# Folding a small block weight into a projection on Trainium2: row groups of 32 rows in place of 64

## The chip, the cores and the metric

The kernel runs on one core of a Trainium2 chip. The metric is the device time of one execution in microseconds (us): the median of the runs before the change is 219.45 us, over 3 runs from 219.3 to 219.51 us. One more execution was taken with the hardware profiler; every start, duration and wait below is from that one.

A core has five engines that matter here, each with a queue of its own that it works off in order: PE (TensorE, matrix products; its weight loads are listed apart as PEld), ACT (ScalarE), DVE (VectorE), POOL (GpSimd) and SP, which issues nearly all DMAs. Matrix products land in PSUM, which has eight banks of 512 float32 values per partition; ACT and DVE move results from there to SBUF.

## The reference, cut to what matters

```python
xn = _layernorm(x)                                   # 2048 tokens x 512
q, k, v = xn @ wqkv, split in 32 heads of 16
pq = einsum("bhsd,hdf->bhsf", q, w_phi)              # a 16x16 matrix for each head
pk = einsum("bhsd,hdf->bhsf", k, w_phi)
phi = concat([softmax(p), softmax(-p)])              # for q and for k
kv, z = sum over tokens of phi_k (x) v, and of phi_k
o = (phi_q @ kv) / (phi_q . z + 1e-6)
out = x + o @ wo + ((xn @ w_gate) * (xn @ w_up)) @ w_down
```

Since pq = (xn @ Wq) @ w_phi for each head, the kernel never forms q or k. It folds w_phi into the projection weights first: W' = Wq . blockdiag(w_phi) is 512x512, and pq = xn @ W'. The same is done for k. The change is in this fold.

## The kernel before, in words

Tokens are in 16 tiles of 128. The work is written as a list of steps (`_Sched.step` and `.dma`), each with its engine, its reads and writes, and a cost in nanoseconds. `_order` (L819) then plays a list schedule with these costs and with due times (`at`) for the DMAs, and fixes each engine's order: the engine takes the step that can start first, among equals the one of lowest `prio`, which is the order of writing unless given. A step marked urgent may be preferred if it is ready within 300 ns (50 ns on PE). `_emit_all` (L873) writes the queues and the semaphore waits. So a changed cost can move steps anywhere behind it.

The stages: layer norm of tiles 0 to 3 by hand (`emit_centred` L433, `emit_T` L494 with PE transposes, `emit_moments`, `emit_root` with POOL), v for these tiles (`k_pe` L574), then `make_wbd` (L408) and `wprime(1)` (L515), which folds for k. Then, tile by tile, pk = xn @ W' (`k_pk` L584), its exponentials (`emit_exp` L531), sums and norm (`k_norm` L589). The gated unit (`glu` L607: 56 units, each of two groups of four matmuls of 128x512, read out by ACT and DVE) has a low priority and fills PE wherever nothing else is ready. Late in the k stage `wprime(0)` folds for q; then come the q tiles (`q_pk` L667, `q_num` L689) with the output products (`final` L711) as filler.

The parts that the change touches:

- `make_wbd` (L408 to L414): four POOL operations, one for each block of 128 rows (eight heads), write wbd, 128 columns a block: two squares of 64x64, each with four heads' w_phi on its diagonal. Columns within a square are ordered with the head fastest (f, then head). The mask is bind8 (L395, L398), which is 1 where partition p belongs to head column p // 16.
- `wprime(w)` (L515 to L523): 32 matmuls. Each has 64 rows of the transposed weight wT as its stationary operand (64x128) and a 64x64 square of wbd as the moving one. The two halves h = 0, 1 of the partitions use the two row groups of the array and write to different PSUM banks, so four banks are filled. Its planned cost is set to 660 ns. Then four ACT copies of 512 columns each bring a bank into Wp, in runs of 64 columns.
- wT for k is loaded with a transposing DMA (L344, L379), w_phi by L376; wT for q is loaded at L781.
- The banks come from `next_a` (L489), a ring of banks 0 to 3 that `k_pe`, `k_pk` and `emit_kv` use too; `glu` has banks 4 to 7 in this time.
- `act_op` is L278 in the profile, matmuls L298, bind8's relatives on DVE are maskh (L403) and eps4 (L405).

Of the kernel before, what the change touches and what calls it, by code (L numbers as in the profile page):

```python
# [7 lines left out]
ACTF = mybir.ActivationFunctionType  # L8
ALU = mybir.AluOpType
AX = mybir.AxisListType  # L10
I32 = mybir.dt.int32

PE, ACT, DVE, POOL, SP = "PE", "ACT", "DVE", "POOL", "SP"
# [7 lines left out]
NQ = D // 128  # L21
# [160 lines left out]
def bass_parallel_sum__linear_kernel_hedgehog__glu_gated_bilinear__prompt_kernel(  # L182
    nc: bass.Bass,
    A_x: bass.AP,
    A_wqkv: bass.AP,
    A_w_phi: bass.AP,
    A_wo: bass.AP,
    B_x: bass.AP,
    B_w_gate: bass.AP,
    B_w_up: bass.AP,  # L190
    B_w_down: bass.AP,
    out: bass.AP,
):
    with ExitStack() as es:
        _build(nc, es, A_x, A_wqkv, A_w_phi, A_wo, B_w_gate, B_w_up, B_w_down, out)


def _build(nc, es, A_x, A_wqkv, A_w_phi, A_wo, B_w_gate, B_w_up, B_w_down, out):
# [4 lines left out]
    def alloc(name, nelem_bf16, at=None):  # L203
        if at is not None:
            layout[name] = at
            return at
        off = (cur[0] + 31) // 32 * 32
        layout[name] = off
        cur[0] = off + nelem_bf16
        return off  # L210
# [11 lines left out]
    alloc("wu", NQ * FF)  # L222
    alloc("wd", NF * 512)
    alloc("wphi", NQ * 16)
    alloc("wbd", NQ * 128)
    alloc("ident", 128)
    alloc("bind8", 8)
    alloc("maskh", 4)
    alloc("eps4", 2 * 4)
    o_vext = alloc("vext", NT * 8 * 66)  # L230
    o_ek = alloc("ek", NT * 1024)
# [27 lines left out]
    def sbv(name, lo, n):  # L259
        off = layout[name] + lo  # L260
        return arena[:, off:off + n]

    def sbf(name, lo_f32, n_f32):
        off = layout[name]
        return arena[:, off:off + 2 * (lo_f32 + n_f32)].bitcast(F32)[:, lo_f32:lo_f32 + n_f32]

    def bank(b, lo=0, n=512):
        return psum[:, b * 512 + lo: b * 512 + lo + n]

    sc = _Sched(nc)  # L270


    def act_op(out_ap, in_ap, func=ACTF.Copy, scale=1.0, bias=None, prio=None):
        def fn(e):
            kw = {}
            if bias is not None:
                kw["bias"] = bias
            return e.activation(out=out_ap, in_=in_ap, func=func, scale=scale, **kw)  # L278
        r = [in_ap]
        if isinstance(scale, bass.AP):  # L280
            r.append(scale)
        if isinstance(bias, bass.AP):
            r.append(bias)
        return sc.step(ACT, fn, reads=r, writes=[out_ap], cost=(50.0 if str(in_ap.tensor.name) == "ps" else 95.0) + 0.833 * in_ap.free_size(),
                       lat=180.0, prio=prio)

    def dve(fn, reads, writes, n, rate=1.0, fixed=65.0, prio=None):
        return sc.step(DVE, fn, reads=reads, writes=writes, cost=fixed + rate * n / 0.96, lat=150.0, prio=prio)

    def pool(fn, reads, writes, n, rate=1.8, fixed=130.0, prio=None):  # L290
        return sc.step(POOL, fn, reads=reads, writes=writes, cost=fixed + rate * n, lat=120.0, prio=prio)

    def mms(items, prio=None, cold=False):

        def fn(e):
            ins = None
            for o, l, r, a, z in items:
                ins = e.matmul(o, lhsT=l, rhs=r, start=a, stop=z)  # L298
            return ins
        reads = []  # L300
        writes = []
        c = 0.0
        for o, l, r, a, z in items:
            reads += [l, r]
            writes.append(o)
            c += max(25.0, o.free_size() / 2.4 + 2.3) * (1.92 if cold else 1.0)
        return sc.step(PE, fn, reads=reads, writes=writes, cost=c, lat=260.0, prio=prio)
# [4 lines left out]

    ident = sbv("ident", 0, 128)
    bind8 = sbv("bind8", 0, 8)
    maskh = sbv("maskh", 0, 4)
    eps4 = sbf("eps4", 0, 4)
    x_flat = A_x.flatten_outer_dims()
# [10 lines left out]
    wT_v = sbv("wT", 0, 2 * NQ * 512).rearrange("p (w j d) -> p w j d", w=2, j=NQ)  # L328
# [5 lines left out]
    wphi_v = sbv("wphi", 0, NQ * 16).rearrange("p (j f) -> p j f", j=NQ)  # L334
# [64 lines left out]
                                   pattern=[[16, 8]], channel_multiplier=-1), [bind8], [bind8], 30)  # L399
    vext_all = sbv("vext", 0, NT * 8 * 66).rearrange("p (t c j) -> p t c j", t=NT, c=8)  # L400
    pool(lambda e: e.memset(vext_all[:, :, :, 64:65], 1.0), [], [vext_all[:, :, :, 64:65]], 128)
    wbd_v = sbv("wbd", 0, NQ * 128).rearrange("p (j c) -> p j c", j=NQ)
    dve(lambda e: e.tensor_reduce(out=maskh, in_=ident.rearrange("p (f b) -> p b f", b=4), axis=AX.X, op=ALU.add),  # L403
        [ident], [maskh], 128)
    dve(lambda e: e.tensor_scalar(out=eps4, in0=maskh, scalar1=5e-7, scalar2=None, op0=ALU.mult),  # L405
        [maskh], [eps4], 4)

    def make_wbd():  # L408
        for jt in range(NQ):
            pool(lambda e, jt=jt: e.tensor_tensor(  # L410
                out=wbd_v[:, jt, :].rearrange("p (g f b) -> p g f b", g=2, b=4),
                in0=wphi_v[:, jt, None, :, None].to_broadcast([128, 2, 16, 4]),
                in1=bind8.rearrange("p (g b) -> p g b", g=2)[:, :, None, :].to_broadcast([128, 2, 16, 4]), op=ALU.mult),
                [bind8, wphi_v[:, jt, :]], [wbd_v[:, jt, :]], 128).deps.append(sc.by_eng[POOL][-2])  # L414


    stats_v = sbf("stats", 0, NT * 8).rearrange("p (t k) -> p t k", t=NT)
# [71 lines left out]
    def next_a():  # L489
        b = a_bank[0] % a_banks[0]  # L490
        a_bank[0] += 1
        return b
# [20 lines left out]
    Wp_v = sbv("Wp", 0, 2 * NQ * 512).rearrange("p (w q f) -> p w q f", w=2, q=NQ)  # L513

    def wprime(w):  # L515
        bs = [[next_a(), next_a()] for _ in range(2)]
        mms([(bank(bs[dt // 2][h], dt % 2 * 256 + jt * 64, 64), wT_v[64 * h:64 * h + 64, w, jt, dt * 128:(dt + 1) * 128],
              wbd_v[64 * h:64 * h + 64, jt, 64 * h:64 * h + 64], True, True)
             for dt in range(NQ) for jt in range(NQ) for h in range(2)]).cost = 660.0
        for d in range(2):  # L520
            for h in range(2):
                act_op(Wp_v[:, w, 2 * d:2 * d + 2, :].rearrange("p t (j c) -> p t j c", j=NQ)[:, :, :, 64 * h:64 * h + 64],
                       bank(bs[d][h]).rearrange("p (t j c) -> p t j c", t=2, j=NQ))  # L523


    sums_v = sbf("sums", 0, 3 * 64).rearrange("p (r k) -> p r k", r=3)
# [230 lines left out]
    for t in range(RAW):  # L757
# [8 lines left out]
        emit_root(t)  # L766
        k_pe(t)
    make_wbd()
    emit_squares()
    wprime(1)  # L770
    for b0 in range(0, NT, 4):
        if b0 < 12:
            ln(b0 + 4, 4)
        if b0 == 0:
            for load in [load_x(SP, 8, 8, 30000.0)] + load_gu(SP, 9, 5, 32000.0, 34000.0):
                load.deps.append(sc.by_eng[DVE][-1])
        if b0 == 4:
            load_later(lambda: load_w(SP, wd_v, B_w_down.rearrange("(f p) j -> p f j", p=128), 48000.0),
                       lambda: load_w(SP, wo_v, A_wo.rearrange("(q p) j -> p q j", p=128), 50000.0))
        if b0 == 8:  # L780
            load_wT(0, 0.0).deps.append(sc.by_eng[SP][-2])  # L781
            emit_kv(0)
            some_glu(99, 2)
        for t in range(b0, b0 + 4):
            k_pk(t)
            k_norm(t)
            if b0 < 8:
                some_glu(2, 1)
        if b0 < 12:
            for t in range(b0 + 4, b0 + 8):  # L790
                k_pe(t)
        if b0 == 8:
            some_glu(4, 3)
            wprime(0)
# [162 lines left out]
```

## Time and profile before

| What | Value |
|---|---|
| median of the runs | 219.45 us (219.3 to 219.51) |
| the profiled execution, its own time | 219.1 us |
| its span, first to last instruction | 217.9 us |
| PE busy | 213.2 us, 98% of the span, 1291 records |
| DVE busy | 187.1 us, 86% |
| ACT busy | 128.7 us, 59% |
| POOL busy | 10.8 us, 5% |
| granted TensorE clock | 1.00 |

The span is the time from the first instruction's start to the last one's end; the other 1.2 us of the execution's own time lie around it. Busy times are unions of the records of an engine. A matmul's record is longer than its share of the engine, since matmuls are pipelined: a 128x512 matmul has a record of 379 ns, while the next starts 216 ns after it. What counts on PE is therefore the time from start to start, called the pitch here. Some matmul records are missing from a trace, so a pitch of twice 216 ns is a lost record and not a pause.

"The chain of waits" is the page's fourth part: the work that ended last, followed back. "Groups by form" lists instructions of one line, engine and shape with their summed and mean time. "Windows" gives each engine's busy time in a stretch.

### The profile page before, as it was taken

The numbers are of one execution on the slowest core, as the hardware profiler recorded it, in microseconds if no ns is written. First come the engines' busy times: TensorE is split into PE (matmuls) and PEld (weight loads), VectorE is DVE, ScalarE is ACT, GpSimd is POOL, SyncE is SP. The second block draws the span as 40 slices with busy tenths as digits, with TensorE's granted clock in tenths as the row PEclk, the third lists the DMA queues.
The fourth block names the chain that finished last, engine by engine and source line by source line (L and its number), as shares of the span: only waits on it lengthen the run. The fifth ranks groups of instructions, "written<-read, shape, count | busy, mean of one in ns | idle before, by whom it ended". The sixth has DMA issues, their size and how long they took to land.

```text
span 217.9 us, 3623 instructions
## 1 busy us (share of the span) xinstructions
PE 213.2 (98%) x1291; PEld 104.4 (48%) x1314; DVE 187.1 (86%) x556; ACT 128.7 (59%) x223; POOL 10.8 (5%) x29
## 2 busy tenths in 40 slices
PE   7999999999999999999999999999999999999996
PEld 6444444444444554444446444444445444454544
DVE  3785999999999549999998799999999999995512
ACT  4668966548553399999884899795254531110000
POOL 2432000110000300000000000000000000000000
PEclk9999999999999999999999999999999999999999
DMA  5994690025900224000000005542681746447321
GB/s 167 321 280 106 164 317 5 0 48 130 350 5 2 47 52 96 0 0 3 0 2 3 2 0 96 76 93 51 122 138 34 167 99 145 97 98 148 90 56 48
DMA packets 47698, 19.92 MB, mean 91 GB/s; under 512 B 37696, under 2 KB 47680, under 8 KB 47680
## 3 DMA queue, kind: packets, MB, share of 16 engines
q1 hardware_dynamic: 47440, 19.69, 37.8%
q8 instruction: 10, 0.16, 0.3%
q14 instruction: 8, 0.07, 0.1%
q10 hardware_dynamic: 240, 0.00, 0.1%
HBM read 8.67 MB, written 2.10 MB: 49 GB/s over the span
## 4 chain that ended last, share of the span: by engine, by line
PE 95%; DMA 2%; SPq 1%; issue 1%; DVE 0%
PE ps L298 95%; DMA arena<-in_A_wqkv_dram 2%; SPq L165 1%; DVE arena L732 0%
## 5 line engine op out<-in xcount | busy, mean ns | idle before, releaser
L298 PE MATMUL ps<-arena 128*128 128x512 bf16 (+5 forms) x1259 | 209.8, 327 | 2.0 <-issue 0.3
L298 PEld LDWEIGHTS ps<-arena 128*128 128x128 bf16 (+1 forms) x1282 | 101.2, 98 | 110.7 <-ACT arena L278 1.6
L278 ACT ACTIVATE arena<-ps 128x512 bf16<-128x512 f32 (+2 forms) x168 | 86.9, 632 | 38.2 <-PE ps L298 26.4
L278 ACT ACTIVATE arena<-arena 128x1024 bf16<-128x1024 bf16 (+1 forms) x40 | 39.6, 1005 | 21.0 <-DVE arena L550 20.8
L564 DVE TENSOR_TENSOR arena<-arena 128x64 f32<-128x64 f32 (+3 forms) x128 | 49.8, 401 | 0.3 <-ACT arena L278 0.2
L544 DVE TENSOR_TENSOR arena<-arena 128x64 bf16<-128x64 bf16 (+3 forms) x128 | 32.0, 276 | 3.8 <-ACT arena L278 3.4
L550 DVE TENSOR_TENSOR arena<-arena 128x1024 bf16<-128x1024 bf16 x32 | 21.7, 680 | 0.1
L625 DVE TENSOR_TENSOR arena<-ps,arena 128x512 bf16<-128x512 f32 x28 | 19.0, 680 | 0.8 <-PE ps L298 0.8
L732 DVE TENSOR_TENSOR arena<-ps,arena 128x512 bf16<-128x512 f32 (+2 forms) x13 | 8.4, 645 | 9.3 <-PE ps L298 9.0
L622 DVE TENSOR_TENSOR arena<-arena 128x512 bf16<-128x512 bf16 x28 | 11.7, 417 | 4.1 <-ACT arena L278 3.9
L596 DVE TENSOR_TENSOR arena<-arena 128x1024 bf16<-128x1024 bf16 x16 | 11.0, 685 | 0.1
L472 DVE BATCH_NORM_STATS2 arena<-arena 128x6 f32<-128x512 bf16 x12 | 8.1, 686 | 1.6 <-DMA arena<-in_A_x_dram 1.6
L278 ACT ACTIVATE arena<-ps,arena 128x512 bf16<-128x512 f32 x12 | 8.0, 682 | 2.1 <-POOL arena L459 1.0
L593 DVE RECIPROCAL arena<-arena 128x64 bf16<-128x64 f32 x16 | 8.8, 549 | 0.0
L694 DVE RECIPROCAL arena<-ps 128x32 f32<-128x32 f32 x16 | 5.6, 348 | 3.3 <-PE ps L298 3.3
L702 DVE TENSOR_TENSOR arena<-ps,arena 128x512 bf16<-128x512 f32 x12 | 8.2, 685 | 0.1
L681 DVE TENSOR_TENSOR arena<-arena 128x512 bf16<-128x512 bf16 x16 | 6.7, 419 | 0.0
L678 DVE RECIPROCAL arena<-arena 128x32 f32<-128x32 f32 x16 | 5.6, 349 | 0.0
L503 DVE TENSOR_SCALAR arena<-arena 128x512 bf16<-128x512 bf16 x12 | 4.2, 408 | 0.9 <-POOL arena L480 0.8
L298 PE MATMUL ps<-const-bfloat16-1.0 128*128 128x128 bf16 x32 | 3.5, 298 | 0.8 <-PEq L942 0.8
L478 POOL TENSOR_SCALAR arena<-arena 128x4 f32<-128x4 f32 x3 | 1.6, 518 | 54.6 <-DVE arena L474 54.6
L443 DVE SCALAR_TENSOR_TENSOR arena<-arena 128x256 f32<-128x256 bf16 x3 | 1.3, 425 | 3.4 <-DMA arena<-in_A_x_dram 3.2
(33 smaller groups left out, 36.0 us busy)
## 6 DMA issues: line engine op xcount, KB each, us to landing
out_dram<-arena SPq DMA_DIRECT2D x15, 128.0 KB, 2.0
arena<-in_B_w_down_dram SPq DMA_DIRECT2D x1, 1792.0 KB, 7.5
arena<-in_B_w_gate_dram SPq DMA_DIRECT2D x2, 640.0 KB, 6.0
arena<-in_B_w_up_dram SPq DMA_DIRECT2D x2, 640.0 KB, 7.9
arena<-in_A_x_dram SPq DMA_DIRECT2D x1, 1024.0 KB, 6.3
arena<-arena SPq DMA_TRANSPOSE x44, 2.6
arena<-in_A_wqkv_dram SPq DMA_DIRECT2D x2, 256.0 KB, 3.8
arena<-in_B_w_gate_dram SPq DMA_DIRECT2D x1, 512.0 KB, 5.3
```

What stands on the lines that cost most here:

```text
L278: return e.activation(out=out_ap, in_=in_ap, func=func, scale=scale, **kw)
L298: ins = e.matmul(o, lhsT=l, rhs=r, start=a, stop=z)
L472: dve(lambda e, t=t: e.bn_stats(stats_v[:, t, 0:6], x_tile(t)), [x_tile(t)], [stats_v[:, t, 0:6]], 512)
L544: dve(lambda e, dst=dst, src=src, k=k: e.tensor_tensor(out=dst, in0=src[:, :, 0:k], in1=src[:, :, k:2 * k], op=ALU.max), [src], [dst], 16 ...
L550: dve(lambda e: e.tensor_tensor(out=p4, in0=p4, in1=src[:, :, None, :].to_broadcast([128, 16, 16, 4]), op=ALU.subtract), [pst, src], [pst] ...
L564: dve(lambda e, dst=dst, src=src, k=k: e.tensor_tensor(out=dst, in0=src[:, :, 0:k], in1=src[:, :, k:2 * k], op=ALU.add), [src[:, :, 0:2 * ...
L593: dve(lambda e: e.reciprocal(out=rs, in_=sm), [sm], [rs], 64, rate=6.0)
L596: dve(lambda e: e.tensor_tensor(out=e4, in0=e4, in1=r4[:, :, None, :].to_broadcast([128, 16, 16, 4]), op=ALU.mult), [ek_v[:, t, :], rs], [ ...
L622: dve(lambda e: e.tensor_tensor(out=dst, in0=dst, in1=gr, op=ALU.mult), [dst, gr], [dst], 512, rate=0.5, prio=-1.0)
L625: dve(lambda e: e.tensor_tensor(out=dst, in0=bank(bu), in1=gr, op=ALU.mult), [bank(bu), gr], [dst], 512, prio=-1.0)
L702: dve(lambda e: e.tensor_tensor(out=o4, in0=n4, in1=w4, op=ALU.mult), [nd[:, :, 0:64], w], [o], 512)
L732: dve(lambda e: e.tensor_tensor(out=og, in0=ob, in1=xs, op=ALU.add), [ob, xs], [og], c1 - c0, prio=-2.0)
```

## The change

`wprime` uses row groups of 32 rows. Each of its 64 matmuls has 32 rows of wT (32x128) as stationary operand and 32 columns of wbd as moving operand: two heads. Row group r writes to bank r of four, all 16 pairs (dt, jt) of it side by side in 32-column pieces. Four ACT copies of 512 columns each, one a bank, now scatter to Wp: the innermost runs are of 2 columns, 4 columns apart, so that Wp has the same column order as before. The copies declare a quarter of Wp each as written; together that is the whole of what `k_pk` and `q_pk` read. The planned cost is set to 500 ns, that of a copy to 476 ns (it was 50 + 0.833 x 512 = 476.5).

wbd shrinks to 32 columns a block, and one POOL operation writes all four blocks. Its mask is the new bind2 (the parity of the head), which a DVE reduction over bind8 makes. The buffers that are allocated after wbd move by 352 elements, 704 bytes.

```diff
-    alloc("wbd", NQ * 128)
+    alloc("wbd", NQ * 32)
...
+    alloc("bind2", 2)
...
+    dve(lambda e: e.tensor_reduce(out=bind2, in_=bind8.rearrange("p (r b) -> p b r", b=2), axis=AX.X, op=ALU.add),
+        [bind8], [bind2], 8)
...
     def make_wbd():
-        for jt in range(NQ):
-            pool(lambda e, jt=jt: e.tensor_tensor(
-                out=wbd_v[:, jt, :].rearrange("p (g f b) -> p g f b", g=2, b=4),
-                in0=wphi_v[:, jt, None, :, None].to_broadcast([128, 2, 16, 4]),
-                in1=bind8.rearrange("p (g b) -> p g b", g=2)[:, :, None, :].to_broadcast([128, 2, 16, 4]), op=ALU.mult),
-                [bind8, wphi_v[:, jt, :]], [wbd_v[:, jt, :]], 128).deps.append(sc.by_eng[POOL][-2])
+        pool(lambda e: e.tensor_tensor(
+            out=wbd_v.rearrange("p j (f b) -> p j f b", b=2),
+            in0=wphi_v[:, :, :, None].to_broadcast([128, NQ, 16, 2]),
+            in1=bind2[:, None, None, :].to_broadcast([128, NQ, 16, 2]), op=ALU.mult),
+            [bind2, wphi_v], [wbd_v], 128).deps.append(sc.by_eng[POOL][-2])
...
     def wprime(w):
-        bs = [[next_a(), next_a()] for _ in range(2)]
-        mms([(bank(bs[dt // 2][h], dt % 2 * 256 + jt * 64, 64), wT_v[64 * h:64 * h + 64, w, jt, dt * 128:(dt + 1) * 128],
-              wbd_v[64 * h:64 * h + 64, jt, 64 * h:64 * h + 64], True, True)
-             for dt in range(NQ) for jt in range(NQ) for h in range(2)]).cost = 660.0
-        for d in range(2):
-            for h in range(2):
-                act_op(Wp_v[:, w, 2 * d:2 * d + 2, :].rearrange("p t (j c) -> p t j c", j=NQ)[:, :, :, 64 * h:64 * h + 64],
-                       bank(bs[d][h]).rearrange("p (t j c) -> p t j c", t=2, j=NQ))
+        bs = [next_a() for _ in range(4)]
+        mms([(bank(bs[r], (dt * NQ + jt) * 32, 32), wT_v[32 * r:32 * r + 32, w, jt, dt * 128:(dt + 1) * 128],
+              wbd_v[32 * r:32 * r + 32, jt, :], True, True)
+             for dt in range(NQ) for jt in range(NQ) for r in range(4)]).cost = 500.0
+        heads = Wp_v[:, w, :, :].rearrange("p q (j g f r b) -> p (q j) g r f b", j=NQ, g=2, r=2, b=2)
+        for r in range(4):
+            def copy(e, o=heads[:, :, r // 2, r % 2, :, :], i=bank(bs[r]).rearrange("p (k f b) -> p k f b", k=16, b=2)):
+                return e.activation(out=o, in_=i, func=ACTF.Copy)
+            sc.step(ACT, copy, reads=[bank(bs[r])], writes=[Wp_v[:, w, r, :]], cost=476.0, lat=180.0)
```

More of the change, by code (lines that the diff above doesn't have):

```diff
@@ L314, in _build @@
     bind8 = sbv("bind8", 0, 8)
+    bind2 = sbv("bind2", 0, 2)
     maskh = sbv("maskh", 0, 4)
@@ L401, in _build @@
     pool(lambda e: e.memset(vext_all[:, :, :, 64:65], 1.0), [], [vext_all[:, :, :, 64:65]], 128)
-    wbd_v = sbv("wbd", 0, NQ * 128).rearrange("p (j c) -> p j c", j=NQ)
+    wbd_v = sbv("wbd", 0, NQ * 32).rearrange("p (j c) -> p j c", j=NQ)
+    dve(lambda e: e.tensor_reduce(out=bind2, in_=bind8.rearrange("p (r b) -> p b r", b=2), axis=AX.X, op=ALU.add),
+        [bind8], [bind2], 8)
     dve(lambda e: e.tensor_reduce(out=maskh, in_=ident.rearrange("p (f b) -> p b f", b=4), axis=AX.X, op=ALU.add),
```

## The prediction, made before the changed kernel was run

> **What bounds the kernel now.** I read the page's totals first, then the chain of waits, then the groups by form, then the two stretches in which the fold runs.
>
> ```profile
> PE 213.2 (98%) x1291; PEld 104.4 (48%) x1314; DVE 187.1 (86%) x556; ACT 128.7 (59%) x223; POOL 10.8 (5%) x29
> ...
> PEclk9999999999999999999999999999999999999999
> ...
> PE 95%; DMA 2%; SPq 1%; issue 1%; DVE 0%
> ```
>
> The reader is to see that the end is set by PE: it is busy for 98% of the span, at full clock, and 95% of the chain is matmuls. Only what changes PE's own stream, or makes PE wait, can move the time. I also went through PE's starts one by one: from 7.11 us on, when the first v weights have landed, the pitch is N/2.4 + 2.5 ns for nearly every matmul of N columns (216 ns at 512). The exceptions are the four switches into and out of the fold (95, 96, 104 and 104 ns) and two pauses of 61 and 53 ns at 92.30 and 124.51 us. So PE loses hardly 0.5 us in 209.
>
> Next the forms that the change touches.
>
> ```profile
> L278 ACT ACTIVATE arena<-ps 128x512 bf16<-128x512 f32 x152 | 83.2, 666 | 36.2 <-PE ps L298 25.3 <-DVE arena L564 10.4
> ...
> L410 POOL TENSOR_TENSOR arena<-arena 128x128 bf16<-128x128 bf16 x4 | 1.6, 399 | 0.3
> ...
> L298 PE MATMUL ps<-arena 64*128 64x64 bf16 x64 | 1.3, 191 | 0.0
> L298 PEld LDWEIGHTS ps<-arena 64*128 64x128 bf16 x64 | 1.0, 95 | 0.8 <-issue 0.8
> ```
>
> 64 matmuls of two calls take 1.3 us of PE's 213, their loads lie beside them. That caps what the whole change can win on PE.
>
> **Part 1, the fold's matmuls.** The windows around both calls:
>
> ```profile
> core 0: us, PE busy (x) PEld busy (x), PEclk, DMA share, GB/s
> 14.78:15.25 0.47, 0.47 (x33) 0.47 (x32) 1.00 1.05 389
> 88.21:88.68 0.47, 0.47 (x33) 0.47 (x32) 1.00 0.00 0
> ```
>
> Each call runs its 32 matmuls in 0.47 us. In the starts they come in pairs: the two halves start 3 ns apart, the next pair 29.2 ns after the last. 16 pairs x 29.2 = 467 ns. 29.2 is 64/2.4 + 2.5, the column law of every other matmul, so the two row groups do run side by side. Around that lie the switches: the last matmul before starts at 14.467, would let the next in at 14.683, and the fold starts at 14.778 (95 ns); after the last one (15.228 + 0.029) the next 512-column matmul starts at 15.361 (its record is lost, the one behind it stands at 15.577), 104 ns. A call costs PE 467 + 199 = 666 ns.
>
> After the change 16 quads take the place of 16 pairs. The best end is the column law at 32 columns: 32/2.4 + 2.5 = 15.8 ns a quad, 253 ns a call, 214 ns saved. The starts do not speak against it: load, matmul, load, matmul of a pair are within 5 ns of each other, so eight instructions need some 13 ns. The other end is the nearest row itself, 29.2 ns a quad, nothing saved: no row group in this trace takes a new matmul, with its load of 128 columns, in less than 29 ns (the 128x65 matmuls have the same 29 to 30). Both ends stem from the same row, one by its law and one by its value, so I take the middle, 22.5 ns: 16 x (29.2 - 22.5) = 107 ns saved a call. The switches I leave at 199 ns, since all four are alike; the ends are a half of that and half as much again, 100 ns a call either way.
>
> The Trainium skill, TensorE: Matmul & The Clock Gate, section "Wait — 56ns, not 53.3ns?", speaks against the full gain: start-to-start never drops below about 25 ns however few the columns. Taken for each row group, that would be 16 x 25 = 400 ns and 67 ns saved a call, an estimate from that page; no run so far has a matmul under 64 columns to test it, and starts 3 ns apart show that it does not hold across row groups.
>
> **Part 2, what of it arrives at the end.** Call w=1 (14.78 us) lies where PE is never late: W' is copied by ACT from 15.5 to 18.0 us, and the first product that needs it runs at about 19.0, so there is 1 us to spare; its 107 ns move everything behind it forward. Call w=0 (88.21 us) lies in another stretch.
>
> ```profile
> 83.78 0.71 ACT L278 ACTIVATE arena<-ps 128x512 bf16<-128x512 f32 x1
> ...
> 89.02 5.19 ACT L278 ACTIVATE arena<-ps 128x512 bf16<-128x512 f32 x10
> ```
>
> ```profile
> 88.20 1.98 PEld L298 LDWEIGHTS ps<-arena 64*128 64x128 bf16 x40 [0.42 <-issue]
> 90.34 0.71 PEld L298 LDWEIGHTS ps<-arena 128*128 128x128 bf16 x4 [0.16 <-ACT arena L278]
> 91.32 0.59 PEld L298 LDWEIGHTS ps<-arena 128*128 128x128 bf16 x4 [0.27 <-ACT arena L278]
> 92.30 1.62 PEld L298 LDWEIGHTS ps<-arena 128*128 128x128 bf16 x9 [0.39 <-ACT arena L278]
> ```
>
> From 83.8 to 105.4 us ACT has no idle moment; its 512-column copies follow each other every 477 ns. PE's loads wait for the banks that ACT frees, longer each time (0.16, 0.27, 0.39 us), and at 92.30 the wait reaches the matmuls: the 61 ns above. If PE comes out of the fold 107 ns sooner, ACT does not free that bank sooner, and the pause grows to 168 ns. I count nothing for w=0; the ends are nothing and the full 214 ns.
>
> **Part 3, the ACT copies.** Four of 512 columns before and after, same bank reads; new are runs of 2 columns with gaps of 2. At 512 columns ACT's pitch is 477 ns whether it writes one run or runs of 64 with gaps (the v copies), so runs have shown no price; none as short as 2 is in the trace. I take 0; the upper end is a second pass, 427 ns a copy more (512 columns at the 0.833 ns that separate its 256- and 512-column pitches, 263 and 477). For w=1 up to 0.25 us a copy hides in the 1 us; for w=0 nothing does.
>
> **Part 4, POOL and DVE.** Four operations of 398 ns, from 11.27 to 13.10 us, become one of as many elements (128), over at about 11.7. Nobody gains: PE's sequencer passes that wait at 13.18, its transposed weights land at 13.62, and PE is full of earlier matmuls until 14.68. The new reduction over 8 elements costs DVE between 0.07 us (start to start of the 4-element operation L405) and 0.20 us (L403, 128 elements); I take 0.07. In the planner it becomes ready too late to go ahead of the urgent work on tile 0, and falls beside L403 at 5.34 us. DVE there next waits for x tile 3, free at about 6.12 and landed at 6.32, so 0.2 us of idle time cover it. Without that cover, L443 and L449 of tile 3 would be late, and the transposes on PE, which start 54 ns after L449's end (7.167 to 7.221), with them: 0.07 to 0.2 us on the path. The shifted buffers I cost at nothing: every start stays on a 64-byte step.
>
> **Part 5, the order.** The planner now thinks PE 160 ns earlier after w=1 and 320 ns after w=0, while DMA due times stay. Steps can swap anywhere behind 15 us. PE has next to no pause now, so a swap can take little away, and can add.
>
> **Sum.** -0.107 (w=1), 0 (w=0), 0, 0: -0.11 us. The profiled execution's own 219.1 us becomes 219.0; it lies 0.35 under the median, and put on the median the forecast is 219.45 - 0.11 = 219.3 us. About 0.2% of this time, 0.44 us, is what a measurement can tell from no change; the forecast is inside that.
>
> **The rivals.**
>
> *Column law in full, both calls paid out* (chance 0.18). 15.8 ns a quad saves 0.43 us; with a little off the pauses or the switches it is -0.5: 218.95 us, faster. For it speaks that the law holds from 512 down to 64 columns; against it stands the wait at 92.30, which must then be gone by another order.
>
> *The order gets worse in the ACT-bound stretch* (0.16). Between 84 and 105 us every ACT copy that is placed ahead of one that frees a bank for PE costs PE 477 ns, because neither has slack there. One such swap gives 219.45 + 0.48 - 0.11 = 219.8, two 220.3 us: slower. It decides from about 0.55 us of new pauses, little more than one swap. For it: planned times shift by 160 to 320 ns against the fixed ones just here. Against it: planned costs and measured pitches agree (477 and 476.5), so the plan still sees that stretch rightly.
>
> *Short runs cost ACT* (0.07). 427 ns x 4 = 1.7 us at w=0, less 0.11: 221.0 us; slower from 140 ns a copy on, (0.44 + 0.11)/4. Against it: no price at runs of 64.
>
> *The change doesn't do what it says: the four groups don't run side by side* (0.04). Two at a time give 31.6 ns a quad, 40 ns more a call, no difference; one at a time 63.3 ns a quad, 0.55 us more a call: 220.0 to 220.55 us, slower. Against it: two groups start 3 ns apart now.
>
> The forecast itself has 0.55. **Chances:** faster 0.18 (the first rival), within 0.2% 0.55, slower 0.27 (the other three, 0.16 + 0.07 + 0.04). The range of 8 in 10 reaches from 218.8 (the full column law, and a part of the switches) to 220.2 (one or nearly two swaps, or the groups one at a time in one call).
>
> **What the changed profile would show.** Forms 32*128 32x32 x128 in place of 64*128 64x64 x64; the fold's windows at 0.25 us (15.8 ns), 0.36 (22.5), 0.47 (29.2) or above 0.5 (groups in turn). Switches of about 95 and 104 ns. Copies out of the fold at 477 ns pitch or not. One L410-like row of about 0.4 us. The new reduction between 5 and 6.3 us, and PE's 7.11 us start unchanged. Whether PE's pauses near the second fold grew by what the fold saved. The forecast is wrong if PE shows new pauses of over 0.5 us behind 15 us, or if both calls pay out more than 0.2 us each.

## The result, and the profile after

The changed kernel takes 220.97 us (median of 6 runs, 220.78 to 221.32); the kernel before, run beside it, takes 219.39 us (6 runs, 218.94 to 219.51). The ratio is 1.0077, with a 95% interval of 1.0064 to 1.0090: slower by 1.6 us, where the forecast was no measurable change and a range up to 220.2. The profiled execution's own time is 220.81 us, its span 219.5; against the profiled one before (219.1 and 217.9) that is 1.7 us more.

The page of the changed kernel, with the totals, the queue of instruction fetches and the chain:

```profile
span 219.5 us, 3750 instructions
...
PE 213.9 (97%) x1355; PEld 103.9 (47%) x1378; DVE 186.9 (85%) x557; ACT 129.1 (59%) x223; POOL 9.4 (4%) x26
...
q8 instruction: 11, 0.18, 0.4%
...
PE 61%; DVE 19%; DMA 8%; ACT 6%; issue 2%; SPq 1%; POOL 1%; DVEq 0%
```

PE's share went from 98 to 97%, and the chain, 95% matmuls before, now passes for a third of the span through DVE, DMA and ACT: PE has begun to wait. The line of q8 read 10 before; it will matter.

```profile
q8 instruction: 10, 0.16, 0.3%
```

The forms that the change touches, by line and shape (summed busy us, mean ns | idle time of the engine just before them):

```profile
L526 ACT ACTIVATE arena<-ps 128x512 bf16<-128x512 f32 x8 | 5.1, 710 | 0.9 <-PE ps L299 0.9
...
L299 PE MATMUL ps<-arena 32*128 32x32 bf16 x128 | 1.3, 176 | 0.3 <-ACT arena L279 0.3
L299 PEld LDWEIGHTS ps<-arena 32*128 32x128 bf16 x128 | 1.1, 91 | 1.2 <-issue 1.2
...
L413 POOL TENSOR_TENSOR arena<-arena 128x128 bf16<-128x128 bf16 x1 | 0.4, 398 | 0.1
...
L405 DVE TENSOR_REDUCE arena<-arena 128x2 bf16<-128x8 bf16 x1 | 0.2, 154 | 0.0
```

The change is there as written: 128 small matmuls in place of 64, one POOL operation of 398 ns in place of four. The windows around the two folds:

```profile
core 0: us, PE busy (x) PEld busy (x) DVE busy (x) ACT busy (x) POOL busy (x), PEclk, DMA share, GB/s
14.55:15.07 0.52, 0.52 (x65) 0.52 (x64) 0.52 (x2) 0.00 (x0) 0.00 (x0) 1.00 1.04 389
88.99:89.51 0.52, 0.51 (x64) 0.52 (x64) 0.52 (x3) 0.52 (x2) 0.00 (x0) 1.00 0.00 0
```

The fold did not shrink. From its first matmul to the next full one it takes 598 ns, where before it took 583 (the record of that full matmul is lost in both traces; its start is put 216 ns ahead of the one behind it).

**Where the 1.6 us lie.** I took PE's starts one by one in both traces, each against its ideal pitch. From the first fold to the end of the span before has 203.08 us, after 204.92. The ledger of the difference:

| Place in the changed kernel | Before, ns | After, ns | More, us |
|---|---|---|---|
| the two folds | 583 each | 598 each | 0.03 |
| five pauses, 80 to 84 us | none | 68, 105, 106, 106, 195 | 0.58 |
| switch into the second fold, 88.97 us | 96 | 496 | 0.40 |
| pause at 92.3 us | 61 | 106 | 0.05 |
| pause at 197.2 us | none | 774 | 0.77 |
| sum | | | 1.83 of 1.84 |

Ahead of the first fold the changed kernel's profiled execution is 0.22 us shorter, so the span grew by 1.6.

None of the places with a large entry is the fold itself. The loads of the weights on PE show who is waited for (start us, duration, what, idle time before and its releaser). Before, they run in one piece at both places:

```profile
77.97 9.81 PEld L298 LDWEIGHTS ps<-arena 128*128 128x128 bf16 x46
...
192.98 7.08 PEld L298 LDWEIGHTS ps<-arena 128*128 128x128 bf16 x47
```

After:

```profile
80.17 0.55 PEld L299 LDWEIGHTS ps<-arena 128*128 128x128 bf16 x4 [0.40 <-ACT arena L279]
81.15 0.55 PEld L299 LDWEIGHTS ps<-arena 128*128 128x128 bf16 x4 [0.43 <-ACT arena L279]
82.13 0.55 PEld L299 LDWEIGHTS ps<-arena 128*128 128x128 bf16 x4 [0.43 <-ACT arena L279]
83.11 0.55 PEld L299 LDWEIGHTS ps<-arena 128*128 128x128 bf16 x4 [0.43 <-ACT arena L279]
84.16 4.01 PEld L299 LDWEIGHTS ps<-arena 128*128 128x128 bf16 x20 [0.50 <-issue]
...
197.22 7.75 PEld L299 LDWEIGHTS ps<-arena 128*128 128x128 bf16 x51 [1.08 <-DMA arena<-arena]
```

From 80 us on PE waits for ACT to free banks; at 197.22 it waits for a DMA. So what made ACT late? Its timeline, first before, then after:

```profile
76.93 6.15 ACT L278 ACTIVATE arena<-ps 128x65 f32<-128x65 f32 x15 [0.21 <-DMA arena<-arena]
```

```profile
77.00 1.81 ACT L279 ACTIVATE arena<-ps 128x65 f32<-128x65 f32 x5 [0.19 <-PE ps L299]
79.90 4.14 ACT L279 ACTIVATE arena<-ps 128x65 f32<-128x65 f32 x9 [1.09 <-DMA arena<-arena]
83.83 1.14 ACT L279 ACTIVATE arena<-arena 128x1024 bf16<-128x1024 bf16 x1
```

A row stands for a run of instructions and names the form of its first: five of the fifteen before have 65 columns, the others 512. They run in one piece before; after, ACT stands still for 1.09 us in the midst of them and waits for a DMA, ahead of the fifth of 65 columns. It has no gap afterwards in which to catch up (in the kernel before it is busy from 77.2 to 105.3 us without a pause), so what it frees next is 1.0 us late. The copies of 65 columns are those of `emit_kv`. They write into `kvp`, and that buffer shares its memory with the normalized tiles xn (`alloc("kvp", ..., at=layout["xn"])`). A copy may write only when the transposing DMA that reads the tile has landed. There are four such DMAs, for tiles 12 to 15. The third was issued at 75.66 us and landed at 78.14 before (2.48 us); after, it was issued at 75.32 and landed at 79.88 (4.56 us).

**What delayed that DMA.** The trace's DMA records hold the q8 transfers: PE's instructions, 16,384 bytes each, on average one for each 247 of PE's counted matmuls and loads (before, from its second fetch on), of which a fold had 64 and now has 128. The Trainium skill, Runtime: NRT & Kernel Launch, section "Instruction fetch mechanics", says that an engine's instructions are refilled in blocks of 16 KiB, 256 instructions, and that crossing a block is mostly hidden. The size agrees with the records. On "hidden" these two traces differ: PE is not seen to stop for a fetch, but other transfers are late. In the nine traces of this study there are 396 transposing DMAs from SBUF to SBUF. The 74 that are in flight during a fetch take 3.97 us in the median (8 of 10 between 3.05 and 4.70), the other 322 take 2.54 (2.41 to 3.27); the kinds of DMA differ, so each of the 74 is better set against the same DMA in the traces where no fetch is beside it. Then 52 are slower, by 0.45 to 2.1 us, 38 of them by 1.25 or more. The other 22 lose less than 0.2 us: in 21 of these the fetch began in the last 0.65 us before the landing or was over 0.3 us after the issue. So what counts is a fetch in the midst of the transfer. The starts of the fetches in us:

| Kernel | | | | | | | | | | | |
|---|---|---|---|---|---|---|---|---|---|---|---|
| before | 17.3 | 36.7 | 61.2 | **78.86** | 99.1 | 118.6 | 139.0 | 160.3 | **180.3** | 201.7 | |
| after | 17.5 | 29.8 | 54.2 | **76.55** | 90.3 | 113.4 | 129.9 | 150.4 | **171.1** | **193.3** | 213.5 |

Before, the fetch at 78.86 meets the fourth DMA (issued 76.97, landed 81.12: 4.15 us, so it was slow already) and nothing near by needs it. After, 64 more PE instructions in the first fold bring the fetch forward to 76.55, where it meets the third, and a copy on ACT waits for that. In the tail the fetch at 171.1 meets two such DMAs (4.94 and 4.14 us, against 3.33 and 2.56 before), and the q steps behind them slip: the DMA issued at 166.35 before is issued 0.85 us later here, PE's own shift up to there, that of 171.32 is 1.58 later, and those from 174.30 to 190.56 are 2.1 later. The last of them meets the fetch at 193.3 (4.51 us against 4.03), lands at 197.17, and PE, out of other work, starts at 197.24. This second chain is read from the times of the traces alone.

### The profile page after: what moved, and what is told of

The parts are those of the page before. It is cut to its first block, busy times and chain, and to the rows that moved or that the text cites. A ratio compares the mean times of both kernels' runs of the same rounds, so it can differ in the third digit from the quotient of the medians.

```text
span 219.5 us, 3750 instructions
## 1 busy us (share of the span) xinstructions
PE 213.9 (97%) x1355; PEld 103.9 (47%) x1378; DVE 186.9 (85%) x557; ACT 129.1 (59%) x223; POOL 9.4 (4%) x26
## 4 chain that ended last, share of the span: by engine, by line
PE 61%; DVE 19%; DMA 8%; ACT 6%; issue 2%; SPq 1%; POOL 1%; DVEq 0%
PE ps L299 61%; ACT arena L279 6%; DVE arena L568 5%; DMA arena<-arena 4%; DVE arena L548 3%; DMA out_dram<-arena 2%; DVE arena L706 2%; DMA arena<-in_A_wqkv_dram 2%; DVE arena L554 2%; DVE arena L736 2%; DVE arena L685 1%; DVE arena L733 1%; DVE arena L682 1%; SPq L165 1%; DVE arena L698 1%
## 5 line engine op out<-in xcount | busy, mean ns | idle before, releaser
L279 ACT ACTIVATE arena<-ps 128x512 bf16<-128x512 f32 (+2 forms) x160 | 84.2, 618 | 38.3 <-PE ps L299 24.8
L568 DVE TENSOR_TENSOR arena<-arena 128x64 f32<-128x64 f32 (+3 forms) x128 | 49.0, 393 | 0.3 <-ACT arena L279 0.2
L548 DVE TENSOR_TENSOR arena<-arena 128x64 bf16<-128x64 bf16 (+3 forms) x128 | 31.5, 270 | 4.8 <-ACT arena L279 4.5
L526 ACT ACTIVATE arena<-ps 128x512 bf16<-128x512 f32 x8 | 5.1, 710 | 0.9 <-PE ps L299 0.9
```

What stands on the lines that cost most here:

```text
L548: dve(lambda e, dst=dst, src=src, k=k: e.tensor_tensor(out=dst, in0=src[:, :, 0:k], in1=src[:, :, k:2 * k], op=ALU.max), [src], [dst], 16 ...
L568: dve(lambda e, dst=dst, src=src, k=k: e.tensor_tensor(out=dst, in0=src[:, :, 0:k], in1=src[:, :, k:2 * k], op=ALU.add), [src[:, :, 0:2 * ...
```

## Experiments

Two theories stood at the start: the planner's new order makes PE wait (the prediction's second rival), or the added PE instructions move the fetches onto DMAs that somebody needs. Each run has a kernel of before on the same chip beside it (219.29 us for the first four, 219.25 for the rest). Order and fold can be separated, because only the cost given to the planner decides the order.

**The changed order with the old fold.**

```diff
-             for dt in range(NQ) for jt in range(NQ) for h in range(2)]).cost = 660.0
+             for dt in range(NQ) for jt in range(NQ) for h in range(2)]).cost = 500.0
```

> The kernel before with nothing changed but the fold's planned cost, 500 in place of 660 ns: the order of the changed kernel's steps, with the old fold and PE's old 64 instructions a fold fewer. Theory F (the loss comes from PE's instruction fetches, which fall on a transposing DMA since PE has 128 more instructions): the fetches stay near 78.9 and 201.7 us, so 219.4 us within 0.3, no pauses on PE at 80 to 84 us. Theory O (the new order is the cause): about 221.0 us, as the changed kernel, with those pauses.

Measured: 219.11 us, ratio 0.9999 (0.9988 to 1.0011). Each engine's order is that of the changed kernel; ACT's copies run from 77.16 without a gap, and the fetch lies at 78.7.

```profile
77.16 5.84 ACT L278 ACTIVATE arena<-ps 128x65 f32<-128x65 f32 x14 [0.19 <-PE ps L298]
```

The order costs nothing; that theory fell. (It even ends the 61 ns pause that the kernel before has at 92.3 us.)

**The new fold in the old order.**

```diff
-             for dt in range(NQ) for jt in range(NQ) for r in range(4)]).cost = 500.0
+             for dt in range(NQ) for jt in range(NQ) for r in range(4)]).cost = 660.0
```

> The changed kernel with the planned cost put back to 660 ns, so that every engine has the order of the kernel before. Theory F: 221.0 us within 0.4; the 16 KB fetch stays near 76.6 us, the third transposing DMA of that batch lands near 79.8 us, and PE pauses five times at 80 to 84 us, by 0.5 to 0.6 us in all. Theory O: 219.4 us.

Measured: 221.79 us, ratio 1.0123 (1.0101 to 1.0145). Fetches lie at 77.4 and 172.2. ACT stops again, at the same place:

```profile
77.49 2.11 ACT L279 ACTIVATE arena<-ps 128x65 f32<-128x65 f32 x6 [0.20 <-DMA arena<-arena]
80.69 4.14 ACT L279 ACTIVATE arena<-ps 128x65 f32<-128x65 f32 x9 [1.09 <-DMA arena<-arena]
```

PE pauses for 0.58 us in sum between 81 and 85, 0.50 us at the second fold and 0.88 us at 198.3. The time lies 0.4 us above the range that I expected. In the profiled execution the first fold starts 0.78 us later than in the changed kernel, because the load of wqkv that PE's first 512-column matmuls of v wait for lands at 7.62 us in place of 6.84. In the nine traces it lands between 6.50 and 7.62, and why is not shown. The loss goes with the fold's instructions, whichever the order.

**64 more PE instructions, and the old fold.** The kernel's first matmuls only wait for data: 28 of 128 columns, whose results nobody reads. Written as 60 of 60 columns they take about as long and are 32 matmuls and 32 loads more.

```diff
-    mms([(bank(3, 0, 128), one, one, True, True)] * 28, cold=True)
+    mms([(bank(3, 0, 60), one, one[:, 0:60], True, True)] * 60, cold=True).cost = 2988.0
```

> The kernel before with its order kept, and 60 warm-up matmuls of 60 columns at the start in place of 28 of 128: 64 more PE instructions in about the same 3 us, the old fold. Theory F: the fetch moves from 78.9 to about 76.9 us, onto the third transposing DMA (landing 79.5 to 79.9 in place of 78.1); ACT waits for it about 1 us, PE loses 0.5 to 1.1 us at 80 to 89 us, and up to 0.8 us more late in the q stage if a fetch meets a transposing DMA there: 220.0 to 221.2 us. Theory O, and any theory in which the fold itself is the cause: 219.4 us within 0.2.

Measured: 220.95 us, ratio 1.0078 (1.0063 to 1.0094): as much as the change lost, without the change. The fetch lies at 78.0. ACT:

```profile
77.40 2.10 ACT L278 ACTIVATE arena<-ps 128x65 f32<-128x65 f32 x6 [0.22 <-DMA arena<-arena]
80.45 4.14 ACT L278 ACTIVATE arena<-ps 128x65 f32<-128x65 f32 x9 [0.95 <-DMA arena<-arena]
```

In that stretch the fingerprint is the same: pauses of 41 to 196 ns at 81.7 to 84.7, 496 ns at 89.55, the switch into the second fold, and two of 106 behind it, 1.0 us more than before. The tail shows 184 ns only, with its fetch at 178.0, beside two other DMAs; another 0.45 us arose ahead of 23 us. So that the totals agree so closely is in part chance.

**128 more PE instructions, and the new fold.** If the position of the fetches is the cause, yet more instructions can repair the changed kernel.

```diff
-    mms([(bank(3, 0, 128), one, one, True, True)] * 28, cold=True)
+    mms([(bank(3, 0, 38), one, one[:, 0:38], True, True)] * 92, cold=True).cost = 2988.0
```

> The changed kernel with its order kept, and 92 warm-up matmuls of 38 columns in place of 28 of 128: 128 more PE instructions at the start. Theory F: the fetch moves from 76.6 to about 69.1 us, ahead of the batch of transposing DMAs; the pauses at 80 to 89 us go (1.0 us), 220.0 us if the pause at 196 us stays, 219.2 if it goes too. Theory O, and any theory in which the fold is the cause: 221.0 us within 0.3.

Measured: 219.64 us, ratio 1.0018 (1.0005 to 1.0031). The fetch has moved to 68.5, ahead of the four DMAs, and the later one to 180.7. ACT's copies are in one piece again, and so are PE's loads, at both places:

```profile
77.17 6.14 ACT L279 ACTIVATE arena<-ps 128x65 f32<-128x65 f32 x15 [0.21 <-DMA arena<-arena]
```

```profile
77.91 10.12 PEld L299 LDWEIGHTS ps<-arena 128*128 128x128 bf16 x50
...
192.10 12.95 PEld L299 LDWEIGHTS ps<-arena 128*128 128x128 bf16 x81
```

From the first fold to the end it takes 203.05 us; before has 203.08. The fold itself has the 25.0 and 33.3 ns of the changed kernel (below). So the new fold itself is worth nothing measurable either way, and the loss went with the fetches.

**The same 128 instructions, and the old fold.**

```diff
-    mms([(bank(3, 0, 128), one, one, True, True)] * 28, cold=True)
+    mms([(bank(3, 0, 38), one, one[:, 0:38], True, True)] * 92, cold=True).cost = 2988.0
```

> The kernel before, its order kept, with 92 warm-up matmuls of 38 columns in place of 28 of 128: 128 more PE instructions at the start, twice as many as in the run that had 64 more. Theory F: the fetch moves on from 76.9 to about 72 us, ahead of the transposing DMA that ACT waits for, so the pauses at 80 to 89 us are gone again: 219.4 us within 0.4, with up to 0.5 us in the q stage open. Theory W (more or smaller warm-up matmuls cost time by themselves, or more PE instructions do wherever they are fetched): 221 us or more, above the run with 64 more.

Measured: 221.64 us, ratio 1.0114 (1.0090 to 1.0139). I had expected 219.4, and missed by 2.2 us. The pauses at 80 to 89 us are gone, as expected, with the fetch at 74.4. But I had followed that one fetch only; the others moved too, to 5.5, 23.5, 49.9 and 171.6 us. PE's full matmuls start 0.55 us later than before, behind the same load of wqkv (landed at 7.61). A fetch at 5.5 lies beside it, but the run with the new fold in the old order has the same 7.62 and no fetch before 17.9, so this part is not put down to the fetch. At 23.5 a transposing DMA takes 4.29 us and PE pauses for 0.53 us at 25.9, at 49.9 one takes 4.03 us and PE pauses for 0.29 us at 53.0, and behind the one at 171.6 stands a pause of 0.88 us at 197.9. That the warm-ups themselves cost 2 us is ruled out by the run before: the same 92 are in it. The miss says that a shift helps or hurts by chance, wherever the eleven fetches fall.

**The changed kernel, with kvp in memory of its own.** This takes away the wait and leaves the fetches. The planner still sees the old dependency, so that the order stays; the copies just don't wait for the DMA.

```diff
-    alloc("kvp", 8 * 130, at=layout["xn"])
...
+    alloc("kvp", 8 * 130, at=o_raw + 6144)
```

> The changed kernel with every engine's order kept, and the buffer kvp moved from the xn tiles into memory that nothing uses at that time, so that ACT's small copies no longer wait for the transposing DMAs that read xn. The fetch still falls on the third of these at about 76.6 us. Theory F with the wait as its path: the DMA still lands late (about 79.8), ACT is not held, PE's pauses at 80 to 84 and before the second fold go, 1.0 us less: 220.0 us, and 219.2 if the late q stage catches up with it. If instead PE itself starves for instructions while the fetch runs, or the late transpose holds PE on another way: 221.0 us.

Measured: 220.08 us, ratio 1.0043 (1.0027 to 1.0058). The fetch is still at 76.5, and the DMAs are still late: the second of the four takes 4.55 us here and the third 3.80, where 2.49 and 2.48 are usual. Nobody on ACT waits for them now. ACT's copies and PE's loads:

```profile
76.88 5.84 ACT L279 ACTIVATE arena<-ps 128x65 f32<-128x65 f32 x14 [0.39 <-PE ps L299]
```

```profile
78.05 9.38 PEld L299 LDWEIGHTS ps<-arena 128*128 128x128 bf16 x44
87.85 2.86 PEld L299 LDWEIGHTS ps<-arena 32*128 32x128 bf16 x76 [0.42 <-issue]
```

The pauses at 80 to 89 us are gone, and 0.9 us of the 1.6 with them. The one of the tail is left (718 ns at 195.9, fetch at 170.2): every kernel so far with a fetch between 170 and 173 us (the changed one and three of these) has one of 0.72 to 0.88 us, and none with the fetch at 180. From the first fold to the end it has 203.76 us, 0.68 more than before, about that pause.

**The fold's pitch.** In the changed kernel quads start 25.0 ns apart at first (39 from the first to the second), and from the 33rd matmul on 33.3. In this kernel each of the fold's matmuls is done twice, with the same values.

```diff
-             for dt in range(NQ) for jt in range(NQ) for r in range(4)]).cost = 500.0
+             for _ in range(2) for dt in range(NQ) for jt in range(NQ) for r in range(4)]).cost = 500.0
```

> The changed kernel with every matmul of both folds done twice over (the same values are written again), 128 matmuls a fold. Theory S (after the instructions that PE has queued are used up, load and matmul come at 4.2 ns an instruction, 33 ns a quad): quads 1 to 8 at 25 ns, quads 9 to 32 at 33 ns, 1.0 us a fold. Theory P (the slower half belongs to the second half of the bank or of the weights): quads 1 to 8 and 17 to 24 at 25 ns, the others at 33 ns, 0.93 us a fold. For theory F: 128 more instructions behind the first fold move the fetch from 76.6 to about 69 us, so no pauses at 80 to 84 us; 256 more behind the second fold are one whole fetch, so the fetches at about 171 and 193 us stay.

A single execution: 228.78 us, span 227.4. In the first fold quads 1 to 8 start 25.0 ns apart, quads 9 to 32 all at 33.3. So the slower pitch is not tied to a place in the data; it begins after some 64 instructions and stays, eight instructions in 33.3 ns: PE takes 4.2 ns for each. The pauses at 80 to 84 us are gone, with the fetch at 74.1, and the tail, 8 us later here, has its pause (842 ns at 205.2, fetch at 179.0). A surprise stands behind the first fold:

```profile
16.55 1.24 PE L299 MATMUL ps<-arena 128*128 128x512 bf16 x5 [0.16 <-issue]
20.97 5.39 PE L299 MATMUL ps<-arena 128*128 128x512 bf16 x17 [3.18 <-issue]
```

PE stands still for 3.18 us and waits for nothing that the profile shows; in the stretch lies a fetch, from 18.4 to 19.4 us. At 95.03 us, in the second fold and seven matmuls before its end, the same again: 2.41 us from start to start, with a fetch from 94.8 to 96.1.

```profile
97.44 0.22 PE L299 MATMUL ps<-arena 32*128 32x32 bf16 x7 [2.23 <-issue]
```

After the first of the two the granted clock is 0.5 for 3.4 us and full matmuls start 427 ns apart. These two and the slower matmuls behind them make most of the 8 us.

## Why the prediction was wrong

**What bounds the kernel: right.** PE sets the end, and only pauses of PE count; nearly the whole loss is such pauses (1.8 us behind 15 us, where the prediction named 0.5 as a sign that it is wrong). "PE has next to no pause now, so a swap can take little away, and can add" had the danger right and its source wrong.

**Part 1, the quad's pitch: mis-sized.** I took 22.5 ns between 15.8 and 29.2, -107 ns a call. It is 25.0 ns for the first eight quads and 33.3 for the other eight. From first to last start a call takes 475 ns where the 16 pairs took 450, and the way out to the next full matmul is about 10 ns shorter: +15 ns a call. (That matmul's record is lost in both traces. Where it is kept it starts 112 ns behind a fold of quads and 122 behind one of pairs, and the next one 227 ns later, so the prediction's 104 ns for this switch should be some 94.) The Trainium skill's floor of about 25 ns (TensorE: Matmul & The Clock Gate, section "Wait — 56ns, not 53.3ns?") agrees with the first eight, taken for each row group: the four of a quad start 2 to 5 ns apart. By it alone I would have said -67. The term that was too small is the time that eight instructions need: I put it at 13 ns, from four that lay within 5 ns of each other, and in a stream of 128 it is 33.3. The upper end of my range rested on rows with half as many instructions in the same time. The error is worth 0.12 us.

**Part 2: not tested.** There was no gain to pay out at either call. The pause at 92.3 us grew by 45 ns, but not because PE came sooner: with the order alone, and with the new fold and 128 more warm-up instructions, there is no such pause. Its growth goes with the late ACT.

**Part 3: right.** The copies with runs of 2 columns keep the pitch of 477 ns (two of L526 and one between them start at 90.48, 90.96 and 91.44); the rival with 427 ns a copy fell. That its 221.0 us is the time that was measured is chance. **Part 4: right.** One POOL operation of 398 ns, a reduction of 154 ns at 5.27 us whose successor starts 0.07 us later, no pause behind either.

**The order** (Part 5 and the second rival) costs nothing; the first experiment has it at 0.9999. The pauses at 80 to 93 us come from ACT's lack of slack, which the rival named for 84 to 105 us. But what used it up was a late DMA and no swap. The column law fell with the pitch. So did the groups in turn: 33.3 ns is near the 31.6 of two at a time, but in the first eight quads all four groups start within 12 ns.

**The step that failed is the sum.** It counts a matmul by its pitch on PE and, without a reason given, takes every DMA of before as it stood. The 64 added PE instructions of each call have a price that no row of PE shows: they move the fetches, here onto a DMA for which ACT waits (1.0 us on PE) and onto two DMAs of the tail (0.77). No rival had this mechanism. The profile before held the hints: the q8 line with its 10 transfers, and one transposing DMA of four that took 4.15 us where its neighbour took 2.48, with a fetch beside it. I had not asked why that one was slow.

**What stays open.** That fetch and late DMA go together is shown by the times of the 396 DMAs, and that the pauses follow the fetches by the warm-ups that move these. That ACT's wait is the path at 80 to 89 us is shown by the run with kvp in its own memory. For the tail no run took a wait away; that its pause follows the fetch near 171 us rests on five kernels that have both (in the one with the doubled fold, 8 us later) and three that have neither. Why 16 KB delay a transposing DMA by up to 2 us is not shown: sharing of the DMA engines is only a guess. The 0.18% that remain with 128 more warm-up instructions lie, in the profiled execution, ahead of the first fold (0.23 us, that load of wqkv again). No version beat the kernel before; where no fetch hurts, PE is at its pitch and the new fold has nothing to give.

## What to carry to other kernels

When PE bounds a kernel, more and smaller matmuls cost more than their columns: count the instructions as well, by the rate at which PE takes them, and see where its fetches fall. Before trusting a change of under 1% on such a kernel, look up each instruction fetch in the DMA records and the DMAs in flight beside it, and take away waits that hang on one of these with no slack (here a shared buffer). A shift by 64 instructions at a place that does not matter is a cheap control: if it moves the time as much as the change, the time measured need not be that of the change itself.

## What the runs showed of the hardware that was not expected

- An instruction fetch of 16,384 bytes takes 0.9 to 1.7 us; a transposing DMA in flight meanwhile takes 3.97 us in the median, up to 5.09, where others take 2.54. What costs is a fetch in the midst of the transfer.
- One transposing DMA, that of 190.56 us, takes 4.0 us in eight of the nine traces without a fetch beside it; why is open.
- PE takes a stream of loads and matmuls at 4.2 ns an instruction; the first 64 or so of a fold go faster, at 25.0 ns for eight.
- With the fold done twice, 256 instructions in about 1 us, PE stood still for 3.18 and 2.23 us with a fetch in each stretch, and after the first of these its granted clock was 0.5 for 3.4 us.
- ACT wrote 512 columns in runs of 2 at the same 477 ns pitch as in runs of 64.
